# Attention scores scaled, masked and reduced a unit at a time; more sums of exponentials on ScalarE; three sums of squares on TensorE

## The chip, the cores and the metric

The kernel runs on one core of a Trainium2 chip. The metric is the device time of one execution in microseconds (us). A measurement gives the median of several executions; one further execution is recorded by the hardware profiler, and all rows below come from that one. Five engines work at the same time, each through its own queue in order: TensorE (PE in the rows; PEld is its weight loads), VectorE (DVE), ScalarE (ACT), GpSimd (POOL) and SyncE (SP). An instruction that waits for another engine holds up everything behind it in its own queue.

## The reference

Three parts follow one another. All arithmetic is float32.

```python
scores = q @ k.T / 8                                # 4 batches, 8 heads, 576 positions, 64 wide
scores = where(mask, scores, -1e9)                  # heads 0-3: the last 32 positions
attn = exp(scores - max(scores))                    # heads 4-7: same position modulo 32, not later
attn = attn / (sum(attn) + 1e-9)
x = attn @ v                                        # reshaped to 2304 tokens x 512

xn = x / sqrt(mean(x * x) + 1e-6) * rms_g
x = (silu(xn @ w_gate) * (xn @ w_val)) @ w_out      # 512 -> 1536 -> 512, weights in float64

logits = x @ w_gate2 + modality_bias[modality_id]   # 8 experts, the largest logit picks one
out = gate * (relu(x @ w1[e]) @ w2[e])              # 512 -> 1024 -> 512 for each token's expert
```

## The kernel before

Attention is cut into 48 *units*, numbered from one here. A unit is one batch, one pair of heads and two to four *tiles* of 128 rows (64 queries of each head). In each batch six strided units (heads 4 to 7; tiles of 54 keys; 4, 4 and 3 tiles) come first, then six local ones (heads 0 to 3; tiles of 96 keys; 4, 4, 3, 3, 2 and 2 tiles). A unit goes through four functions. `scores` multiplies on TensorE (L168), scales, masks and takes the row extremum on VectorE (L178, one instruction a tile, each with a readout of the extremum), and exponentiates on ScalarE (L188, one a tile). `norm` sums the exponentials on VectorE (L205; from the 13th unit on, ScalarE's exponential also gives the sum), adds 1e-9 (L206), takes the reciprocal (L207) and multiplies (L208). `transpose` goes through TensorE and ScalarE (L214, L216), and `output` multiplies by v (L224) and copies into x (L233, L239). The values are kept negated, so that the extremum is a minimum.

The feed-forward part works on nine *chunks* of 256 tokens. `rms` squares the chunk on ScalarE (L299), adds the four 128-channel parts on VectorE (L303, L304), sums over channels on TensorE against a column of ones (`root`, L317), finds the reciprocal root with a dozen small VectorE instructions (L323 to L331), spreads it (L337, L339) and scales x (L349 to L353). Then come the gate and value products (L456 to L458), the activation (L464 to L470) and the output product (L481 to L483), for each chunk and each of twelve blocks `f`.

The 36 float64 weight blocks are *converted* on the chip, numbered from one here. Each is loaded by ScalarE's queue (L379); one conversion then takes a copy on ScalarE (L387), a sign step on GpSimd (L389), two VectorE steps (L396, L400), a cast on ScalarE (L408) and a subtraction on VectorE (L409). Buffers are passed on from block to block, so that GpSimd's step of a conversion waits until L396 of the one before has read its block: L389 and L396 form a loop.

The first 24 units and the chunks are put together by hand: the program runs units until eight outputs are done, then `rms` of the first chunk, then a *flow* of (chunk, block) steps, first chunk one alone for three steps, then chunks one and two in turn, then the others. Between the steps come `slot` calls, which hand out one weight load, one conversion half and one piece of attention. What order the instructions then have on each engine is decided by a scheduler that goes by estimated durations, up to the last part (the experts), whose order is written out by hand. In the first 50 us short filler products (L117) run on TensorE as well.

Of the kernel before, what the change touches and what calls it, by code (L numbers as in the profile page):

```python
# [15 lines left out]
AF = mybir.ActivationFunctionType  # L16
# [30 lines left out]
def moe_kernel(  # L47
# [53 lines left out]
    def bank(tag, bufs=1):  # L101
        return ps.tile([128, 512], F32, tag=tag, name=tag, bufs=bufs)
# [8 lines left out]
    n_load = [0, 0]  # L111
    n_out = [0]

    def fill(dst, n):

        for _ in range(n):
            T.matmul(dst, ones16, ones16, start=True, stop=True)  # L117
# [29 lines left out]
    def attention(u, banks):  # L147

        b, p, g = units[u]
        local = p < 2  # L150
        n, t0, nq, nk = geometry(u)
        k0 = n * nq if local else n * nq + LQ - SQ
        st = {}

        def scores():
            t = qkv_t.pop((u, 0))
            pr = pp.tile([128, 4, LK], F32, tag="pr", name="pr", bufs=3)
            mx = sm.tile([128, 4], F32, tag="mx", name="mx")
            sd = sm.tile([128, 4], F32, tag="sd", name="sd")
            sps = banks("s")  # L160
            if n_fill[0] < 16:
                n_fill[0] += 1
                fill(sps[:, 384:], 10)
            sps = sps[:, :4 * LK].rearrange("p (t k) -> p t k", k=LK)
            for i in range(n):
                for h in range(2):
                    hp = slice(64 * h, 64 * h + 64)
                    T.matmul(  # L168
                        sps[hp, i, :nk],
                        t[hp, i * nq:i * nq + LQ],  # L170
                        t[hp, k0 + i * nq:k0 + i * nq + nk],
                        start=True,
                        stop=True,
                    )
            for i in range(n):
                mask = m_str if not local else (m_loc0 if g == 0 and i == 0 else m_loc)
                pv = pr[:, i, :nk]
                V.tensor_tensor_reduce(  # L178
                    out=pv,
                    in0=sps[:, i, :nk],  # L180
                    in1=mask[:, :nk],
                    op0=ALU.add,
                    op1=ALU.min,
                    scale=-0.125,
                    scalar=3.0e38,
                    accum_out=mx[:, i:i + 1],
                )
                act = A.activation(  # L188
                    out=pv,
                    in_=pv,  # L190
                    func=AF.Exp,
                    bias=mx[:, i:i + 1],
                    scale=-1.0,
                    accum_out=None if u < 12 else sd[:, i:i + 1],
                )
                if not flow_on:
                    mark[0] = act
            st["p"] = pr, sd
            load_part(0)

        def norm():
            pr, sd = st["p"]
            pv, sl = pr[:, :n, :nk], sd[:, :n]
            if u < 12:
                V.tensor_reduce(out=sl, in_=pv, op=ALU.add, axis=AX.X)  # L205
            V.tensor_scalar(out=sl, in0=sl, scalar1=1e-9, scalar2=None, op0=ALU.add)  # L206
            V.reciprocal(out=sl, in_=sl)  # L207
            V.tensor_tensor(out=pv, in0=pv, in1=sl.unsqueeze(2).to_broadcast([128, n, nk]), op=ALU.mult)  # L208

        def transpose():  # L210
            pr, _ = st.pop("p")
            pt = banks("t").rearrange("p (t k) -> p t k", k=128)
            for i in range(n):
                T.transpose(pt[:nk, i], pr[:, i, :nk], ident)  # L214
            ptS = st["t"] = pp.tile([128, 4, 128], F32, tag="ptS", name="ptS", bufs=2)
            A.copy(ptS[:nk, :n], pt[:nk, :n])  # L216

        def output():
            t = qkv_t.pop((u, 1))
            ptS = st.pop("t")  # L220
            ot = banks("o")
            for i in range(n):
                for h in range(2):
                    T.matmul(  # L224
                        ot[64 * h:64 * h + 64, i * nq:(i + 1) * nq],
                        t[:nk, i, 64 * h:64 * h + 64],
                        ptS[:nk, i, 64 * h:64 * h + nq],
                        start=True,
                        stop=True,
                    )  # L230
            if local:
                x = x_t[b, p, g] = xt_p.tile([128, n * LQ], F32, tag=f"x{g}", name=f"x{g}", bufs=2)
                A.copy(x, ot[:, :n * LQ])  # L233
            else:
                if g == 0:
                    x_t[b, p] = xt_p.tile([128, S], F32, tag="xs", name="xs", bufs=4)
                x = x_t[b, p].rearrange("p (j c) -> p c j", c=CLS)
                c0, c1 = 3 * t0, min(3 * (t0 + n), CLS)
                A.copy(x[:, c0:c1], ot[:, :(c1 - c0) * LEN].rearrange("p (c j) -> p c j", j=LEN))  # L239
            load_part(1)  # L240
            n_out[0] = u + 1


        if local and b > 0:
            output.after = (S * (b - 1) + LQ * (t0 + n) - 1) // CH
        elif not local and b > 1:
            output.after = (S * (b - 1) - 1) // CH
        return scores, norm, transpose, output
# [42 lines left out]
    def rms(j):  # L291

        st = {}
# [5 lines left out]
                    A.activation(out=sq[:, p % 2, o:o + n], in_=src, func=AF.Square)  # L299

        def add():
            sq = [st.pop(("s", q)) for q in range(2)]
            V.tensor_tensor(out=sq[0], in0=sq[0], in1=sq[1], op=ALU.add)  # L303
            V.tensor_tensor(out=sq[0][:, 0], in0=sq[0][:, 0], in1=sq[0][:, 1], op=ALU.add)  # L304
            st["sq"] = sq[0][:, 0]
# [6 lines left out]
        def root():  # L312


            ss = bank("mx") if j else bank("gv", 2)
            for m in range(2):
                T.matmul(  # L317
                    ss[:, m:m + 1], st["sq"][:, m * 128:(m + 1) * 128], ones[:, 0:1], start=True, stop=True
                )
            a = sm.tile([128, 2], F32, tag="na", name="na")  # L320
            r = sm.tile([128, 2], F32, tag="nr", name="nr")
            t = sm.tile([128, 2], F32, tag="nt", name="nt")
# [814 lines left out]
def _constants():  # L1137
    c = np.zeros((128, 6, 128), np.float32)
    r, k = np.arange(128)[:, None], np.arange(128)[None, :]
    q = r % LQ  # L1140
    loc = (k > q) & (k <= q + WIN)
    c[:, 0] = np.where(loc & (k >= WIN), 0, -8e9)
    c[:, 1] = np.where(loc, 0, -8e9)
    c[:, 2] = np.where((q // LEN == k // LEN) & (k <= q), 0, -8e9)
    c[:, 3] = np.eye(128)
    c[:, 4] = 1
    c[:, 5] = r < k
    i = np.zeros((128, NCOL + 2 * E + 1), np.float32)
    i[:, :NCOL] = np.arange(NCOL)
    i[:, NCOL:NCOL + E] = np.arange(E) * NT  # L1150
    i[:, NCOL + E] = np.arange(1, 129)
    n = r // 32 * E
    i[:, NCOL + E + 1:] = r % 32 == n + np.arange(E)
    return [c.reshape(128, -1), i]
# [82 lines left out]
```

## Time and profile before

| | |
|---|---|
| median of 3 executions | 892.23 us (891.48 to 894.1) |
| the profiled execution, its time | 890.73 us |
| span from its first to its last instruction | 889.0 us |
| busy: PE, DVE, ACT, POOL | 855.3, 532.3, 401.1, 129.4 us |
| mean granted TensorE clock, as a share of 2.4 GHz | 0.976 |

Busy times are shares of the whole span and hide that stages differ, so the rows below are cut by stretch. Between the profiled time and its span lie 1.7 us; the profiled execution is 1.5 us under the median.

### The profile page before, as it was taken

Reading aid. Unit: us, or ns where it says so; the run is one execution under the profiler, and the core shown is the slowest. Engines: PE = TensorE matmul, PEld = TensorE weight load, DVE = VectorE, ACT = ScalarE, POOL = GpSimd, SP = SyncE. Lnnn points to the kernel's source line nnn. Section 1 sums busy time; section 2 is a strip of 40 time slices with the busy share of each in tenths; the row PEclk is TensorE's granted clock in tenths of the full one; section 3 lists DMA queues with packets and bytes.
Section 4 is the critical chain, followed back from the end, with each engine's and each line's share of the span. In section 5 each row is a group of like instructions: output and inputs, shape, how many; then the busy total and the mean of one; then the engine's idle time right before and its main releaser. Section 6 shows DMA issues by size and latency. Waiting matters only on the chain.

```text
span 889.0 us, 18174 instructions
## 1 busy us (share of the span) xinstructions
PE 855.3 (96%) x6912; PEld 770.8 (87%) x6912; DVE 532.3 (60%) x1650; ACT 401.1 (45%) x971; POOL 129.4 (15%) x86
## 2 busy tenths in 40 slices
PE   8569899999999999999999999999999999999996
PEld 7458799999898889888989999998999999999995
DVE  4899999456463564553543635447596666666651
ACT  4665777334454344433232322225365545544540
POOL 1466455000000000000000000001031111111100
PEclk9759999999999999999999999999999999999998
DMA  6936611002211111200000000005187742775000
GB/s 196 361 114 261 229 51 52 10 6 71 61 45 48 40 29 36 68 24 8 25 10 24 1 1 25 1 25 213 42 323 228 223 154 83 231 222 189 25 25 19
DMA packets 33015, 84.47 MB, mean 95 GB/s; under 512 B 5122, under 2 KB 12850, under 8 KB 32920
## 3 DMA queue, kind: packets, MB, share of 16 engines
q1 hardware_dynamic: 24216, 54.89, 19.8%
q10 hardware_dynamic: 5184, 18.88, 5.7%
q0 software_dynamic: 3520, 9.45, 3.2%
q8 instruction: 58, 0.95, 0.5%
q14 instruction: 37, 0.30, 0.1%
HBM read 91.58 MB, written 10.49 MB: 115 GB/s over the span
## 4 chain that ended last, share of the span: by engine, by line
PE 72%; issue 9%; DMA 5%; DVE 3%; POOL 1%; SPq 0%; ACT 0%; POOLq 0%; DVEq 0%
PE gv L456 11%; PE gv L457 11%; PE gv L458 10%; DMA stg<-in 5%; PE o L481 4%; PE o L483 4%; PE o L482 4%; PE o L998 3%; PE o L1000 3%; PE o L999 3%; PE mx L224 2%; PE s L168 2%; PE s L975 1%; PE s L974 1%; PE s L976 1%
## 5 line engine op out<-in xcount | busy, mean ns | idle before, releaser
L456 PE MATMUL gv<-xh,wf 128*128 128x256 f32 x864 | 249.5, 290 | 1.7 <-DVE t L466 1.2
L457 PE MATMUL gv<-xl,wf 128*128 128x256 f32 x864 | 245.1, 284 | 0.0
L458 PE MATMUL gv<-xh,wf 128*128 128x256 f32 x864 | 244.8, 283 | 0.0
L456 PEld LDWEIGHTS gv<-xh,wf 128*128 128x128 f32 x864 | 163.2, 189 | 9.2 <-DVE t L466 1.8
L457 PEld LDWEIGHTS gv<-xl,wf 128*128 128x128 f32 x864 | 163.3, 189 | 3.9 <-issue 0.2
L458 PEld LDWEIGHTS gv<-xh,wf 128*128 128x128 f32 x864 | 163.6, 189 | 0.3
L941 DVE TENSOR_TENSOR l<-stg,h 128x1024 fp32r<-128x1024 f32 x88 | 107.1, 1223 | 37.3 <-ACT h L940 37.1
L465 DVE SCALAR_TENSOR_TENSOR t<-t,gv 128x256 f32<-128x256 f32 x108 | 45.1, 418 | 115.5 <-ACT t L464 114.8
L940 ACT CAST h<-stg 128x1024 fp32r<-128x1024 f32 x88 | 91.6, 1048 | 35.1 <-PE o L1000 25.9
L464 ACT ACTIVATE t<-gv 128x256 f32<-128x256 f32 x108 | 41.3, 382 | 143.0 <-PE gv L458 131.6
L389 POOL TENSOR_SCALAR wk<-raw 128x512 int32<-128x512 f32 x36 | 78.5, 2179 | 77.9 <-DVE wk L396 27.1
L481 PE MATMUL o<-wf,hh 128*128 128x512 f32 x192 | 76.9, 401 | 1.2 <-ACT hh L469 1.2
L482 PE MATMUL o<-wf,hh 128*128 128x512 f32 x192 | 75.9, 395 | 0.0
L483 PE MATMUL o<-wf,hl 128*128 128x512 f32 x192 | 75.3, 397 | 0.2 <-DVE hl L470 0.2
L469 ACT CAST hh<-t 128x256 fp32r<-128x256 f32 x108 | 43.7, 405 | 69.0 <-PE o L483 29.9
L998 PE MATMUL o<-h,hT 128*128 128x512 f32 x176 | 70.6, 401 | 0.0
L1000 PE MATMUL o<-h,hT 128*128 128x512 f32 x176 | 68.8, 391 | 0.0
L999 PE MATMUL o<-l,hT 128*128 128x512 f32 x176 | 68.5, 389 | 0.0
L924 POOL DMA_INDIRECT xg<-rows_d,gi x22 | 24.3, 1105 | 301.7 <-DMA stg<-in 141.2
L470 DVE TENSOR_TENSOR hl<-t,hh 128x256 fp32r<-128x256 f32 x108 | 47.1, 436 | 34.8 <-ACT hh L469 34.4
L188 ACT ACTIVATE pr<-pr,mx 128x54 f32<-128x54 f32 (+1 forms) x160 | 52.5, 346 | 19.3 <-DVE mx L178 17.3
L974 PE MATMUL s<-xh,h 128*128 128x256 f32 x176 | 49.7, 282 | 0.0
(208 smaller groups left out, 1636.3 us busy)
## 6 DMA issues: line engine op xcount, KB each, us to landing
stg<-in SPq DMA_DIRECT2D x96, 512.0 KB
raw<-in ACTq DMA_DIRECT2D x36, 512.0 KB
rows_d<-x SPq DMA_DIRECT2D x18, 256.5 KB
qk<-in SPq DMA_DIRECT2D x16, 221.0 KB
qk<-in SPq DMA_DIRECT2D x8, 272.0 KB
v<-in SPq DMA_DIRECT2D x16, 108.0 KB
qk<-in SPq DMA_DIRECT2D x8, 208.0 KB
v<-in SPq DMA_DIRECT2D x8, 192.0 KB
```

What stands on the lines that cost most here:

```text
L389: G.tensor_scalar(out=wk[:, 1], in0=raw[:, :, 1].bitcast(F32), scalar1=0.0, scalar2=-(2.0**31), op0=ALU.is_lt, op1=ALU.mult,)
L456: T.matmul(dst, wh[:, ks], xh[k], start=(k == order[0]), stop=False)
L457: T.matmul(dst, wh[:, ks], xl[k], start=False, stop=False)
L458: T.matmul(dst, wl[:, ks], xh[k], start=False, stop=(k == order[3]))
L481: T.matmul(o, h[:, ms], wh, start=(f == 0), stop=False)
L482: T.matmul(o, h[:, ms], wl, start=False, stop=False)
L483: T.matmul(o, l[:, ms], wh, start=False, stop=(f == NF - 1))
L940: A.copy(h, lt["stg", i])
L941: V.tensor_tensor(out=l, in0=lt["stg", i], in1=h.bitcast(F32), op=ALU.subtract)
L998: T.matmul(ys[t][m], hh, w[0][:, c], start=(q == 0 and c == 0), stop=False)
L999: T.matmul(ys[t][m], hh, w[1][:, c], start=False, stop=False)
L1000: T.matmul(ys[t][m], hl, w[0][:, c], start=False, stop=(q == 3 and c == 1))
```

## The change

Three edits:

- `scores`: scaling and masking is one VectorE instruction for all tiles of a unit that share a mask (two for the first local unit of each pair of heads), and the row minima of the unit are one further instruction. No instruction a tile with readout is left. The mask tables hold 1e9 instead of -8e9 accordingly.
- `norm`: ScalarE's exponential also gives the sum from the seventh unit on (before, from the 13th), and L205 goes for the seventh to twelfth unit. From the seventh unit on the 1e-9 is added by ScalarE instead of VectorE.
- `rms`: for the first three chunks the VectorE additions go, and TensorE sums the four parts, with four products for each half of the chunk in place of one.

```diff
+    NRED = 6
...
+            m0 = 1 if local and g == 0 else 0
+            for i0, i1, mask in ((0, m0, m_loc0), (m0, n, m_loc if local else m_str)):
+                if i0 < i1:
+                    V.scalar_tensor_tensor(
+                        out=pr[:, i0:i1, :nk], in0=sps[:, i0:i1, :nk], scalar=-0.125,
+                        in1=mask[:, :nk].unsqueeze(1).to_broadcast([128, i1 - i0, nk]),
+                        op0=ALU.mult, op1=ALU.add,
+                    )
+            V.tensor_reduce(out=mx[:, :n], in_=pr[:, :n, :nk], op=ALU.min, axis=AX.X)
             for i in range(n):
-                mask = m_str if not local else (m_loc0 if g == 0 and i == 0 else m_loc)
                 pv = pr[:, i, :nk]
-                V.tensor_tensor_reduce(
-                    out=pv,
-                    in0=sps[:, i, :nk],
-                    in1=mask[:, :nk],
-                    op0=ALU.add,
-                    op1=ALU.min,
-                    scale=-0.125,
-                    scalar=3.0e38,
-                    accum_out=mx[:, i:i + 1],
-                )
...
-                    accum_out=None if u < 12 else sd[:, i:i + 1],
+                    accum_out=None if u < NRED else sd[:, i:i + 1],
...
-            if u < 12:
+            if u < NRED:
                 V.tensor_reduce(out=sl, in_=pv, op=ALU.add, axis=AX.X)
-            V.tensor_scalar(out=sl, in0=sl, scalar1=1e-9, scalar2=None, op0=ALU.add)
+                V.tensor_scalar(out=sl, in0=sl, scalar1=1e-9, scalar2=None, op0=ALU.add)
+            else:
+                A.activation(out=sl, in_=sl, func=AF.Copy, bias=1e-9)
...
         def add():
+            if j < 3:
+                return
...
+            if j < 3:
+                sq = [st["s", q][:, i] for q in range(2) for i in range(2)]
+            else:
+                sq = [st["sq"]]
             for m in range(2):
-                T.matmul(
-                    ss[:, m:m + 1], st["sq"][:, m * 128:(m + 1) * 128], ones[:, 0:1], start=True, stop=True
-                )
+                for i, a in enumerate(sq):
+                    T.matmul(
+                        ss[:, m:m + 1], a[:, m * 128:(m + 1) * 128], ones[:, 0:1],
+                        start=(i == 0), stop=(i == len(sq) - 1),
+                    )
```

The scheduler orders the changed program anew, most of all on VectorE and ScalarE in the first 100 us. In the rows below, line numbers of the changed kernel are its own: L181 and L186 are the new scaling and minima, L209 is ScalarE's addition of 1e-9; L210, L211, L398, L407, L411, L419, L420 and L334 are L207, L208, L387, L396, L400, L408, L409 and L323 of before.

On VectorE, where the tenth to twelfth unit are normalized and the fifth and sixth conversion pass, there stands before, from L400 of the fifth conversion to L396 of the sixth:

```order
L400 SCALAR_TENSOR_TENSOR wk<-wk 128x512
L207 RECIPROCAL sd<-sd 128x3
L409 TENSOR_TENSOR wf<-wk,wf 128x512
L206 TENSOR_SCALAR sd<-sd 128x2
L208 TENSOR_TENSOR pr<-pr,sd 128x288
L205 TENSOR_REDUCE sd<-pr 128x2
L207 RECIPROCAL sd<-sd 128x2
L396 SCALAR_TENSOR_TENSOR wk<-raw,wk 128x512
```

and now, from L407 of the fifth conversion to that of the sixth:

```order
L407 SCALAR_TENSOR_TENSOR wk<-raw,wk 128x512
L210 RECIPROCAL sd<-sd 128x3
L211 TENSOR_TENSOR pr<-pr,sd 128x288
L210 RECIPROCAL sd<-sd 128x2
L211 TENSOR_TENSOR pr<-pr,sd 128x192
L411 SCALAR_TENSOR_TENSOR wk<-wk 128x512
L420 TENSOR_TENSOR wf<-wk,wf 128x512
L210 RECIPROCAL sd<-sd 128x2
L211 TENSOR_TENSOR pr<-pr,sd 128x192
L420 TENSOR_TENSOR wf<-wk,wf 128x512
L407 SCALAR_TENSOR_TENSOR wk<-raw,wk 128x512
```

L396 of the sixth conversion stood ahead of the subtraction (L409) of the fifth and of the last reciprocal; now L407 stands behind all reciprocals and products of these units and behind the subtractions of the fourth and the fifth.

On ScalarE, in the same place, there stands before, from the last load of a group to the cast after the 12th unit's exponentials:

```order
L379 DMA raw<-in 128x1024 x3
L188 ACTIVATE pr<-pr,mx 128x96 x2
L408 CAST wf<-wk 128x512
L387 ACTIVATE wk<-raw 128x512
L188 ACTIVATE pr<-pr,mx 128x96 x2
L233 COPY x_656<-mx 128x256
L216 COPY ptS<-o_783 96x384
L408 CAST wf<-wk 128x512
```

and now, from the 11th unit's last exponential to the next cast but one:

```order
L189 ACTIVATE pr,sd<-pr,mx 128x96
L209 ACTIVATE sd<-sd 128x2
L189 ACTIVATE pr,sd<-pr,mx 128x96
L398 ACTIVATE wk<-raw 128x512
L419 CAST wf<-wk 128x512
L236 COPY x_641<-mx 128x256
L219 COPY ptS<-o_769 96x384
L209 ACTIVATE sd<-sd 128x2
L398 ACTIVATE wk<-raw 128x512
L419 CAST wf<-wk 128x512
```

The copy of the sixth conversion (L387) stood ahead of the 12th unit's exponentials; now the copies of the fifth and of the sixth (L398) both stand behind them. The reciprocal on VectorE now waits for L209, which for the 12th unit stands behind a conversion's copy and cast and two other copies.

On VectorE, where the squares of the first chunk are added, there stands before:

```order
L400 SCALAR_TENSOR_TENSOR wk<-wk 128x512
L409 TENSOR_TENSOR wf<-wk,wf 128x512
L396 SCALAR_TENSOR_TENSOR wk<-raw,wk 128x512
L303 TENSOR_TENSOR sq<-sq 128x512
L400 SCALAR_TENSOR_TENSOR wk<-wk 128x512
L304 TENSOR_TENSOR sq<-sq 128x256
L178 ISA pr,mx<-pt,cs 128x54
L178 ISA mx 128x1
...
L409 TENSOR_TENSOR wf<-wk,wf 128x512
L396 SCALAR_TENSOR_TENSOR wk<-raw,wk 128x512
L323 TENSOR_SCALAR na<-gv 128x2
```

and now, up to the same small instruction of `root`:

```order
L407 SCALAR_TENSOR_TENSOR wk<-raw,wk 128x512
L411 SCALAR_TENSOR_TENSOR wk<-wk 128x512
L420 TENSOR_TENSOR wf<-wk,wf 128x512
L407 SCALAR_TENSOR_TENSOR wk<-raw,wk 128x512
L181 SCALAR_TENSOR_TENSOR pr<-pt,cs 128x4x54
L411 SCALAR_TENSOR_TENSOR wk<-wk 128x512
L186 TENSOR_REDUCE mx<-pr 128x4
L420 TENSOR_TENSOR wf<-wk,wf 128x512
L407 SCALAR_TENSOR_TENSOR wk<-raw,wk 128x512
L334 TENSOR_SCALAR na<-gv 128x2
```

The two additions are gone, and between the last two conversions ahead of `root` two instructions of the 13th unit stand in place of eight. On TensorE the sum over channels is four rows of L317 for each of the first three chunks before and sixteen now.

## Rows read from the trace of the kernel before

**Rows 1.** Busy time by stretch: PE, PEld, DVE, ACT, POOL, granted clock, DMA share, GB/s

```profile
25.00:50.00 25.00, 13.30 (x157) 10.92 (x158) 20.25 (x75) 16.67 (x44) 12.60 (x6) 0.67 0.97 352
...
75.00:100.00 25.00, 21.87 (x184) 18.91 (x183) 24.20 (x64) 15.95 (x39) 15.20 (x7) 1.00 0.67 257
...
125.00:150.00 25.00, 25.00 (x230) 22.55 (x230) 23.65 (x63) 18.26 (x52) 14.42 (x7) 1.00 0.17 48
```

**Rows 2.** Timeline of PE: start us, us, operation, idle before and releaser

```profile
50.18 1.23 PE L117 MATMUL pt<-ones 128*128 128x128 bf16 x10 [4.93 <-ACT ptS L216]
...
53.41 1.02 PE L317 MATMUL gv<-cs,sq 128*128 128x1 f32 x4 [0.97 <-DVE sq L304]
...
76.45 0.38 PE L456 MATMUL gv<-xh,wf 128*128 128x256 f32 x1 [0.91 <-DVE t L466]
...
102.09 0.39 PE L456 MATMUL gv<-xh,wf 128*128 128x256 f32 x1 [0.33 <-DVE t L466]
```

**Rows 3.** Timeline of DVE: maxima of a unit and sums of exponentials

```profile
8.28 0.21 DVE L178 CUSTOM_DVE_ANT_0 pr<-s,cs 128x54 f32<-128x54 f32 x1
8.41 0.08 DVE L178 DVE_READ_ACCUMULATOR2_ANT mx<- 128x1 f32 x1
8.41 0.21 DVE L178 CUSTOM_DVE_ANT_0 pr<-s,cs 128x54 f32<-128x54 f32 x1
...
18.86 0.37 DVE L205 TENSOR_REDUCE sd<-pr 128x4 f32<-128x216 f32 x1
...
30.13 0.55 DVE L205 TENSOR_REDUCE sd<-pr 128x4 f32<-128x384 f32 x1
30.59 0.17 DVE L207 RECIPROCAL sd<-sd 128x4 f32<-128x4 f32 x1
```

**Rows 4.** Groups by shape: busy us, mean ns, idle before and releaser

```profile
L465 DVE SCALAR_TENSOR_TENSOR t<-t,gv 128x256 f32<-128x256 f32 x108 | 45.1, 418 | 115.5 <-ACT t L464 114.8
...
L206 DVE TENSOR_SCALAR sd<-sd 128x4 f32<-128x4 f32 x24 | 4.5, 189 | 8.0 <-ACT pr L188 7.9
```

**Rows 5.** Timeline of DVE around the squares of the first chunk

```profile
51.28 0.68 DVE L303 TENSOR_TENSOR sq<-sq 128x512 f32<-128x512 f32 x1
...
52.94 0.41 DVE L304 TENSOR_TENSOR sq<-sq 128x256 f32<-128x256 f32 x1
...
54.41 0.68 DVE L396 SCALAR_TENSOR_TENSOR wk<-raw,wk 128x512 int32<-128x512 int32 x1
55.01 0.15 DVE L323 TENSOR_SCALAR na<-gv 128x2 f32<-128x2 f32 x1
```

**Rows 6.** Instructions of L317 in the first chunk: duration min/median/max, starts

```profile
L317 PE MATMUL gv<-cs,sq x4: 352/353/373, 53.4 to 54.1; 128*128 128x1 f32 x4
```

**Rows 7.** Timeline of PE: the same sum of squares in the third chunk

```profile
178.73 0.50 PE L317 MATMUL mx<-cs,sq 128*128 128x1 f32 x4
179.09 0.36 PE L456 MATMUL gv<-xh,wf 128*128 128x256 f32 x1
```

**Rows 8.** Timeline of POOL: its step of the sixth to ninth conversions

```profile
39.53 1.94 POOL L389 TENSOR_SCALAR wk<-raw 128x512 int32<-128x512 f32 x1 [1.04 <-DVE sd L206]
44.27 2.29 POOL L389 TENSOR_SCALAR wk<-raw 128x512 int32<-128x512 f32 x1 [2.79 <-DVE wk L396]
48.25 2.39 POOL L389 TENSOR_SCALAR wk<-raw 128x512 int32<-128x512 f32 x1 [1.69 <-DVE wk L396]
51.51 2.27 POOL L389 TENSOR_SCALAR wk<-raw 128x512 int32<-128x512 f32 x1 [0.87 <-DVE wk L396]
```

**Rows 9.** Timeline of ACT between 40 and 54 us

```profile
40.48 0.64 ACT L188 ACTIVATE pr<-pr,mx 128x96 f32<-128x96 f32 x2 [1.70 <-DMA raw<-in]
...
48.20 0.67 ACT L387 ACTIVATE wk<-raw 128x512 f32<-128x512 f32 x1 [1.42 <-DVE wk L396]
...
53.58 0.34 ACT L188 ACTIVATE pr<-pr,mx 128x54 f32<-128x54 f32 x1
...
53.91 0.32 ACT L188 ACTIVATE pr<-pr,mx 128x54 f32<-128x54 f32 x1
```

More of the change, by code (lines that the diff above doesn't have):

```diff
@@ L1141, in _constants @@
     loc = (k > q) & (k <= q + WIN)
-    c[:, 0] = np.where(loc & (k >= WIN), 0, -8e9)
-    c[:, 1] = np.where(loc, 0, -8e9)
-    c[:, 2] = np.where((q // LEN == k // LEN) & (k <= q), 0, -8e9)
+    c[:, 0] = np.where(loc & (k >= WIN), 0, 1e9)
+    c[:, 1] = np.where(loc, 0, 1e9)
+    c[:, 2] = np.where((q // LEN == k // LEN) & (k <= q), 0, 1e9)
     c[:, 3] = np.eye(128)
```

## Prediction

> **What bounds the kernel now.** I read the table of stretches first: it says in which part of the span a saving can count at all. From 125 us on TensorE is busy for the whole of each stretch up to 570 us, the first of which stands here, and VectorE, though busy for 23.65 of 25 us between 125 and 150 us, holds nobody up [rows 1]. Only TensorE's own work has a price there. Between 75 and 100 us VectorE is busy for 24.20 of 25 us and TensorE for 21.87: here VectorE sets the pace [rows 1]. Between 25 and 50 us neither is full; the DMA engines are, at 0.97 of their share [rows 1]. So a VectorE saving must fall before about 102 us, where the timeline of TensorE has its last idle time: from 53.41 to 102.09 us eleven rows of that view begin after an idle time, the first of 0.97 us, the last of 0.33 us, 7.7 us in all [rows 2]. That is the most that the stretch of the flow can give back; the 4.93 us before 50.18 us come on top and belong to the head [rows 2].
>
> The second thing to see is what the head waits for. ScalarE's queue is held by weight loads until 40.48 us and by a VectorE step of a conversion at 48.20 us [rows 9], and the conversions form a loop with GpSimd: its steps start at 39.53, 44.27, 48.25 and 51.51 us, and the idle time before the last three ends with VectorE's L396 [rows 8]. The shortest of these periods, 3.26 us, is about GpSimd's 2.3 us and L396's 0.68 us with hand-overs [rows 5, 8], so I take it as the loop's floor. The first small step of the first chunk's root (L323, 55.01 us) stands directly behind the ninth conversion's L396, which begins at 54.41 us [rows 5].
>
> **The change part by part.** The sum is made against the profiled execution, 890.73 us, 1.50 us under the median.
>
> *Maxima.* Two tiles' instructions start 0.13 us apart, and the readout between them takes no time of its own [rows 3]: four tiles of 54 cost 0.53 us. A reduction of 384 columns hands over after 0.46 us although it lasts 0.55, so 0.09 us are a tail that overlaps; that of 216 columns, 0.37 us, then costs 0.28 us [rows 3]. The new scaling reads PSUM and SBUF as L465 does, 0.418 us for 256 columns [rows 4]; 40 columns less at the (0.55 - 0.37) / 168 = 1.07 ns of the reductions give 0.375 us, 0.29 us without the tail. So a strided unit of four tiles costs 0.57 us instead of 0.53, one of three 0.46 instead of 0.39; a local unit of four 0.9 to 1.0 instead of 0.70 (a tile of 96 is 0.13 us plus 42 columns, 0.175 us). The edit adds VectorE time, because every column is now read twice. In the VectorE-bound stretch (65 to 102 us) three units are scored: +0.2 us.
>
> The Trainium skill (Vector Engine (DVE) Microarchitecture Reference, Measured stream behaviour on trn2) states about 75 ns for each instruction after queue overlap and 1.0417 ns a column. By it the readouts, of one column each, would cost 76 ns apiece, and eleven of them in this stretch would make the edit save 0.6 us instead of costing 0.2, and the total 0.8 us less. The trace disagrees on the readouts, whose start coincides with that of the next tile [rows 3], and agrees on the slope with 1.07 ns.
>
> *Sums.* Six L205 of the seventh to twelfth unit go, 0.46 us and less each [rows 3], all in the head, where VectorE is not full. ScalarE pays for them: two exponentials with sums start 0.33 us apart for 54 columns [rows 9], and eighteen of the tiles now have sums. By the slope above a local one costs some 0.36 us. The addition of 1e-9 leaves VectorE for 42 units: 0.189 us long, less the tail 0.10 us [rows 4]; four of them between 65 and 102 us, -0.4 us.
>
> *Squares.* VectorE is spared 0.59 + 0.32 us, the two rows without their tails, for each of three chunks [rows 5]. TensorE gets twelve more passes a chunk. At full clock four take 179.09 - 178.73 = 0.36 us [rows 7], so twelve cost 1.08 us; in the first chunk four starts spread over 0.7 us [rows 6], at the half clock that the page's slices show there, and twelve cost 2.5 us or a little less.
>
> *Head, up to the first gate product.* Here the order decides. Before, ScalarE left its wait at 40.48 us and GpSimd's seventh step began at 44.27 us, 3.8 us later [rows 8, 9]. The new order puts one chain between them: four exponentials with sums (1.44 us), three copies of sums (0.4), a load's issue (0.3), then for the fifth conversion copy, shift, cast and subtraction and for the sixth L407 (five steps of 0.6 to 0.68 us, taken like L396), together 5.4 us: GpSimd would begin at 45.9 us. From there the loop has no squares, no L205 and fewer instructions in it; I take the floor: steps at 49.1 and 52.4 us, the ninth L407 2.3 us later, at 54.7 us instead of 54.41. The sixteen passes over the first chunk are not later than that: the last square comes some 0.5 us earlier than before, since one conversion less stands ahead of it, and seven products of two passes take 2.9 us. Head: +0.3 us. Bounds: all lateness kept, +1.6 us; or the two long periods before (4.74 and 3.98 us) shrink to the floor as well, -2.2 us. Units one to six only get latency of about 0.4 us each, under DMA that is full soon after: 0, with 1 us on either side.
>
> *Flow, 65 to 102 us.* VectorE: -0.9 (squares of chunk two) - 0.4 + 0.2 = -1.1 us. TensorE's 1.08 us for chunk two fall where it waited 0.91 us for VectorE [rows 2], and cost 0.2 us. Bounds: with the contention that stretches some VectorE rows, -2.1 us; hidden behind GpSimd's loop, 0; the passes in full, +1.1 us.
>
> *Chunk three* is squared at 178 us, where TensorE never idles: +1.1 us. Later units cost VectorE more and the chain from scores to products some 0.7 us more, but between a unit's scores and its transposes the order leaves TensorE 8 us and more of other work; 0, and that is what would pay if the cover went.
>
> Sum: 0 + 0.3 - 1.1 + 0.2 + 1.1 = +0.5 us, that is 891.2 us profiled and 892.7 us as a median. The low ends add up to -4.2 us, the high ends to +4.8 us.
>
> **The rivals.** All times are medians.
>
> *Faster: the loop runs at its floor.* VectorE no longer stands in wait for exponentials ahead of a reduction, and if ScalarE is not the later one, both long periods shrink (-2.2), the flow gives -2.1 with the extra passes hidden, and chunk three takes 1.1 back: -3.2 us, 889.0 us. For it speaks that all idle time before GpSimd's steps ended with VectorE [rows 8]; against it, that the new order moves the fifth and sixth copies on ScalarE behind the exponentials.
>
> *Slower: ScalarE becomes the bound of the head.* ScalarE is busy for 16.67 us between 25 and 50 us and held by loads besides [rows 1, 9], and gets some 2.5 us more. A reciprocal then waits for a tiny copy behind a cast, and the conversion's step stands behind the reciprocal. The 1.6 us stay, the passes of chunks two and three cost 2.2 us in full, and the flow gains nothing: +3.8 us, 896.0 us. It decides if GpSimd's seventh step begins later than about 46 us.
>
> *The edit on VectorE doesn't do what it says.* By the prices above, eight instructions fewer a unit are no time saved; in all 48 units the maxima cost VectorE some 8 us more than before. That is in the forecast; by the rule on instructions it would be 0.8 us better, the same case.
>
> **How the numbers follow.** About 0.3% (2.7 us) is what a measurement of this kernel can tell from no change, so "no change" means 889.6 to 894.9 us. I give it 0.38, the faster rival 0.33 and the slower 0.29: the terms are small and of both signs, and the order of the first 60 us, which no row of before shows, can move the result by several us either way. The likeliest case by itself is 890 to 895 us. The range that leaves out a tenth on either side reaches past both rivals, near the sums of the ends: 887.8 to 897.0 us.
>
> **What would show it.** Right: L181 of 216 columns lasts about 0.37 us and VectorE's total changes little; GpSimd's seventh step at 45 to 46.5 us and L334 within 1 us of 55; TensorE's idle time after 53 us down by about 1 us; 1.4 us for the sixteen passes of chunk three. Wrong: TensorE's clock back at full well before or after the slices in which it was before, idle time of TensorE after 102 us, L407 waiting for ScalarE in every period, or loads that land elsewhere because ScalarE issues them in another order.

## The result, and the profile after

The changed kernel takes 898.79 us (median of 4 executions, 898.41 to 901.5) against 892.57 us for the kernel before, measured beside it: a ratio of 1.0078 with a 95% interval of 1.0057 to 1.0098. A second series gave 899.89 against 892.67 us, 1.0086 [1.0068, 1.0104]. Taken from the ratios, as all differences of runs below, that is 7.0 and 7.7 us slower (the medians differ by 6.2 and 7.2). The forecast was 892.7 us, its range 887.8 to 897.0 us: the measured time lies above it. The two profiled executions stand further apart than the medians, 901.5 and 890.73 us: the changed kernel's lies 2.7 us above its median, that of before 1.8 us under. So differences between single rows are read with some 4 us in mind, and what is held against them comes from several runs.

The table of stretches of the changed kernel answers to [rows 1]; its columns are the same.

```profile
75.00:100.00 25.00, 23.79 (x189) 21.66 (x189) 22.18 (x54) 14.61 (x37) 14.71 (x7) 1.00 0.66 257
100.00:125.00 25.00, 21.31 (x179) 19.18 (x178) 21.54 (x46) 15.64 (x51) 12.61 (x7) 0.86 0.53 185
```

Between 75 and 100 us TensorE is now busy for 23.79 us instead of 21.87, as VectorE's relief was to bring. But between 100 and 125 us it is busy for 21.31 us (before: 23.46) at a granted clock of 0.86 (before: 1.00). The first small step of each chunk's root, a fixed place in the program, tells how late the kernel is. On the timeline of VectorE these are, for chunks one to three:

```profile
57.94 0.15 DVE L334 TENSOR_SCALAR na<-gv 128x2 f32<-128x2 f32 x1
81.85 0.15 DVE L334 TENSOR_SCALAR na<-mx 128x2 f32<-128x2 f32 x1
189.07 0.16 DVE L334 TENSOR_SCALAR na<-mx 128x2 f32<-128x2 f32 x1 [0.77 <-PE mx L327]
```

In the trace of before they begin at 55.01 [rows 5], 79.02 and 179.27 us, and that of chunk four at 249.94 us (now 260.32). The changed kernel is 2.9 us late at chunk one, 2.8 at chunk two, 9.8 at chunk three and 10.4 at chunk four. The traces show two losses, then: 2.9 us in the head, and 7 us between 82 and 189 us. TensorE's timeline (start, us, operation, idle before and releaser) answers to [rows 2] and shows both:

```profile
52.56 3.15 PE L327 MATMUL gv<-cs,sq 128*128 128x1 f32 x14
...
73.06 0.41 PE L469 MATMUL gv<-xh,wf 128*128 128x256 f32 x1
78.81 1.84 PE L327 MATMUL mx<-cs,sq 128*128 128x1 f32 x16
...
95.62 0.28 PE L469 MATMUL gv<-xh,wf 128*128 128x256 f32 x1
...
104.24 0.56 PE L170 MATMUL pt<-qk 64*64 64x54 f32 x12 [1.66 <-DVE pr L181]
106.83 0.58 PE L467 MATMUL gv<-xh,wf 128*128 128x256 f32 x1 [2.03 <-DVE t L477]
107.64 0.41 PE L467 MATMUL gv<-xh,wf 128*128 128x256 f32 x1
...
187.20 1.84 PE L327 MATMUL mx<-cs,sq 128*128 128x1 f32 x16
```

Counted are the gate and value products that read xh. The fifth, at 73.06 us, began at 69.50 us before: 3.6 us late. The 93rd is only 2.5 us late (100.87 against 98.36 us), the 97th 4.7 us (106.83 against 102.09 [rows 2]), behind two idle times of 1.66 and 2.03 us, and from there a product takes 0.41 us in place of 0.28. Short stretches show the clock (columns as in the table above):

```profile
102.00:106.00 4.00, 1.14 (x34) 0.88 (x29) 3.67 (x8) 1.29 (x3) 3.12 (x2) 0.95 0.69 206
106.00:110.00 4.00, 3.17 (x15) 3.17 (x16) 2.95 (x8) 3.19 (x13) 0.53 (x1) 0.50 1.01 385
110.00:114.00 4.00, 4.00 (x21) 3.65 (x21) 3.81 (x9) 1.76 (x5) 2.01 (x2) 0.70 0.94 358
```

TensorE was busy for 1.14 of the 4 us from 102 us on, and then got the half clock, 1.2 GHz: (0.05 + 0.50 + 0.30) x 4 = 3.4 us of full clock gone. Before, the clock was 1.00 throughout this stretch. What TensorE waited for is L477, the end of a block's activation. VectorE's queue ahead of it:

```profile
100.06 0.69 DVE L407 SCALAR_TENSOR_TENSOR wk<-raw,wk 128x512 int32<-128x512 int32 x1 [1.57 <-POOL wk L400]
...
103.20 0.69 DVE L407 SCALAR_TENSOR_TENSOR wk<-raw,wk 128x512 int32<-128x512 int32 x1 [0.29 <-POOL wk L400]
103.81 0.38 DVE L181 SCALAR_TENSOR_TENSOR pr<-pt,cs 128x216 f32<-128x216 f32 x1
104.10 1.12 DVE L420 TENSOR_TENSOR wf<-wk,wf 128x512 fp32r<-128x512 f32 x1
105.15 0.41 DVE L476 SCALAR_TENSOR_TENSOR t<-t,gv 128x256 f32<-128x256 f32 x1
105.48 0.68 DVE L411 SCALAR_TENSOR_TENSOR wk<-wk 128x512 int32<-128x512 int32 x1
106.08 0.36 DVE L186 TENSOR_REDUCE mx<-pr 128x4 f32<-128x216 f32 x1
106.37 0.41 DVE L477 TENSOR_TENSOR t<-t,gv 128x256 f32<-128x256 f32 x1
```

The activation (L476, L477) stands behind L407 of the 21st conversion, which waits for GpSimd, and L420 of the 20th, and L411 of the 21st stands between its two steps. In the trace of before the 20th's subtraction (L409) has begun at 99.55 us, ahead of the activation, and one step of the 21st (L396) stands between the two:

```profile
100.16 0.41 DVE L465 SCALAR_TENSOR_TENSOR t<-t,gv 128x256 f32<-128x256 f32 x1
...
101.02 0.68 DVE L396 SCALAR_TENSOR_TENSOR wk<-raw,wk 128x512 int32<-128x512 int32 x1
101.63 0.41 DVE L466 TENSOR_TENSOR t<-t,gv 128x256 f32<-128x256 f32 x1
```

In the changed kernel the activation's first step on ScalarE stands behind the cast of the 20th conversion:

```profile
102.44 0.62 ACT L419 CAST wf<-wk 128x512 fp32r<-128x512 f32 x1 [0.82 <-DVE wk L411]
102.96 0.38 ACT L475 ACTIVATE t<-gv 128x256 f32<-128x256 f32 x1
```

Of the head, GpSimd's sixth to ninth step, ScalarE ahead of the seventh and around the last square (answers to [rows 8, 9]), and VectorE directly ahead of the root's first step:

```profile
44.61 2.45 POOL L400 TENSOR_SCALAR wk<-raw 128x512 int32<-128x512 f32 x1 [4.10 <-ACT wk L398]
48.32 2.39 POOL L400 TENSOR_SCALAR wk<-raw 128x512 int32<-128x512 f32 x1 [1.26 <-DVE wk L407]
51.59 2.39 POOL L400 TENSOR_SCALAR wk<-raw 128x512 int32<-128x512 f32 x1 [0.87 <-DVE wk L407]
54.85 1.95 POOL L400 TENSOR_SCALAR wk<-raw 128x512 int32<-128x512 f32 x1 [0.87 <-DVE wk L407]
```

```profile
41.53 0.37 ACT L189 ACTIVATE pr<-pr,mx 128x96 f32<-128x96 f32 x1 [0.99 <-DMA qk<-in]
...
42.63 0.33 ACTq L390 DMA_DIRECT2D raw<-in  x1
43.06 0.38 ACT L189 ACTIVATE pr<-pr,mx 128x96 f32<-128x96 f32 x1 [0.62 <-DVE sd L210]
...
51.52 0.68 ACT L398 ACTIVATE wk<-raw 128x512 f32<-128x512 f32 x1 [1.32 <-issue]
52.11 0.40 ACT L302 ACTIVATE sq<-x 128x256 f32<-128x256 f32 x1
```

```profile
57.34 0.68 DVE L407 SCALAR_TENSOR_TENSOR wk<-raw,wk 128x512 int32<-128x512 int32 x1
```

The loop does run at its floor from the seventh step on (3.27 and 3.26 us), but that step comes at 48.32 us (before: 44.27, forecast: 45.9), and the last square now stands behind a conversion's copy.

### The profile page after: what moved, and what is told of

The parts are those of the page before. It is cut to its first block, busy times and chain, and to the rows that moved or that the text cites. A ratio compares the mean times of both kernels' runs of the same rounds, so it can differ in the third digit from the quotient of the medians.

```text
span 899.4 us, 17989 instructions
## 1 busy us (share of the span) xinstructions
PE 867.2 (96%) x6948; PEld 781.5 (87%) x6948; DVE 529.6 (59%) x1380; ACT 406.2 (45%) x1031; POOL 129.1 (14%) x86
## 4 chain that ended last, share of the span: by engine, by line
PE 75%; issue 9%; DMA 1%; POOL 1%; DVE 1%; SPq 0%; ACT 0%; POOLq 0%; DVEq 0%
PE gv L467 11%; PE gv L468 11%; PE gv L469 10%; PE o L494 5%; PE o L492 5%; PE o L493 4%; PE o L1009 3%; PE o L1011 3%; PE o L1010 3%; PE mx L227 2%; PE s L170 2%; PE s L985 2%; PE s L986 2%; PE s L987 2%; PE gv L985 2%
## 5 line engine op out<-in xcount | busy, mean ns | idle before, releaser
L476 DVE SCALAR_TENSOR_TENSOR t<-t,gv 128x256 f32<-128x256 f32 x108 | 45.3, 419 | 110.5 <-ACT t L475 109.6
L400 POOL TENSOR_SCALAR wk<-raw 128x512 int32<-128x512 f32 x36 | 77.8, 2160 | 83.7 <-DVE wk L407 28.7
```

## The experiments

All ratios are to the kernel before, measured beside it, with a 95% interval. In the diffs a line with - is of the kernel that the text names as the base; they are shortened, and `...` marks what is left out.

**One edit alone.** Base: the kernel before. The first theory was that ScalarE's new work costs (A), the rival that VectorE's new order and double reading do (B).

```diff
+V.scalar_tensor_tensor(out=pr[:, i0:i1, :nk], in0=sps[:, i0:i1, :nk], scalar=-0.125, ...)
+V.tensor_reduce(out=mx[:, :n], in_=pr[:, :n, :nk], op=ALU.min, axis=AX.X)
...
-V.tensor_tensor_reduce(out=pv, in0=sps[:, i, :nk], in1=mask[:, :nk], ...)
```

> The kernel before with the maxima edit alone (one scaling and one reduction a unit). Theory A (ScalarE's new work is what costs): this edit adds nothing to ScalarE, so the first full run of gate products starts within 1 us of before (69.5 us in the trace) and the time within 0.3% of before, +0.2 to +0.6 us. Theory B (the new order on VectorE is what costs, every column being read twice there): two thirds of the loss are here, +4 us or more, with gate products 2 us or more later than before.

Measured: 893.15 us, 1.0002 [0.999, 1.0014]. No difference: theory B fell. The fifth of the products that read xh begins at 71.28 us, 1.8 us late, between what the two theories expected. VectorE is busy for 539.3 us instead of 532.3, so the edit does cost it time, 7 us where the forecast had some 8 for all units, but none that counts.

```diff
+NRED = 6
...
-accum_out=None if u < 12 else sd[:, i:i + 1],
+accum_out=None if u < NRED else sd[:, i:i + 1],
...
-if u < 12:
+if u < NRED:
     V.tensor_reduce(out=sl, in_=pv, op=ALU.add, axis=AX.X)
-V.tensor_scalar(out=sl, in0=sl, scalar1=1e-9, scalar2=None, op0=ALU.add)
+    V.tensor_scalar(out=sl, in0=sl, scalar1=1e-9, scalar2=None, op0=ALU.add)
+else:
+    A.activation(out=sl, in_=sl, func=AF.Copy, bias=1e-9)
```

> The kernel before with the sums edit alone (sums of the 7th to 12th unit by the exponential, 1e-9 added by ScalarE from the 7th unit on). Theory A: most of the loss is here, +3.5 to +6 us; VectorE's reciprocal of the 8th or 9th unit waits 2 us or more for ScalarE's addition, and the gate products start 2.5 to 4 us later than before. Theory B: VectorE has less to do and nothing is lost, -1 to +1 us.

Measured: 891.1 us, 0.9994 [0.9981, 1.0008]. Theory A fell: no loss.

```diff
+if j < 3: return
...
+sq = [st["s", q][:, i] for q in range(2) for i in range(2)]
```

> The kernel before with the squares edit alone (sixteen passes of TensorE for each of the first three chunks, no additions on VectorE). Both theories: head and gate start as before within 1 us; +1.1 us for chunk three, +0.2 to +1.1 for chunk two, -0.9 to 0 for VectorE's additions: +0.3 to +2.2 us. If a third cause is at work, TensorE held by passes in the stretch where it runs at half clock, gate products start 1 us or more later and the time is +3 us or more.

Measured: 897.98 us, 1.0065 [1.005, 1.0081], +5.8 us. Both theories fell, and the clause on a third cause was met in its numbers (the fifth product begins at 73.37 us, 3.9 us late): the squares edit carries the loss. That passes at the half clock are this cause isn't shown by it; the runs by chunk below speak against it.

**The changed kernel again**, unchanged.

> The changed kernel once more, for a second profile: the profiled execution lay 2.7 us above the other three. If the second stretch of half clock (105.6 to 112.4 us) comes with the order of instructions, it is there again and the time is 898 to 899 us or more; if it hangs on the one execution, TensorE's idle time of 1.7 and 2.0 us at 104 and 107 us or the half clock behind it is gone in this profile, and its span is 896 to 897 us.

Measured: 899.89 us. The second half-clock stretch is there again, from 105.1 to 111.9 us, and the idle times are 1.66 and 2.04 us: they come with the order.

**The squares edit taken back.** Base: the changed kernel.

```diff
-if j < 3:
+if j < 0:
```

> The changed kernel with the squares edit alone taken back (maxima and sums edits stay). If the squares edit is the whole cause, whatever stands beside it, the 7.2 us go: 892 to 893.5 us, and the gate products start within 1.5 us of before. If the edits only cost together (three edits crowd ScalarE and VectorE in the head), half of the loss or more stays, 896 us or more.

Measured: 893.63 us, 1.0013 [1.0002, 1.0023]. The loss goes but for 1.2 us, and the fifth product begins at 69.35 us, as before. Of the two other edits together that is what stays. Where it arises wasn't followed up; the trace has a granted clock of 0.61 between 101 and 105 us, where that of before has 1.00.

**Squares by chunk.** Base: the kernel before with the squares edit for all three. Theory C put the loss on the first chunk's passes, theory D on chunks two and three.

```diff
-if j < 3:
+if j == 0:
```

> The kernel before with the squares edit for the first chunk alone. Theory C (the twelve more passes of the first chunk stand on the head's chain at half clock, and the root's small steps then fall behind conversions): +3 to +4.5 us, with the spreading product and the gate products 3.5 to 4.5 us later than before. Theory D (the loss is the price of the passes where TensorE never idles, chunks two and three): -0.5 to +1 us.

Measured: 893.46 us, 1.0011 [1.0002, 1.002]. The gate products are 4.8 us late in the trace, but the time is only 1.0 us up (3.3 us between the two profiled executions): lateness in the head doesn't stand in the time in full.

```diff
-if j < 3:
+if j in (1, 2):
```

> The kernel before with the squares edit for the second and third chunk alone. Theory C: the rest, +1 to +2.5 us, of which 1.1 to 1.9 at the third chunk. Theory D: +4 us or more, with the gate products of the first chunk starting as before.

Measured: 899.51 us, 1.0086 [1.0073, 1.0099]. Theory C fell.

For the first chunk alone, with the halves added on VectorE (base: the run of the first chunk alone):

```diff
+V.tensor_tensor(out=sq[0], in0=sq[0], in1=sq[1], op=ALU.add)
...
-sq = [st["s", q][:, i] for q in range(2) for i in range(2)]
+sq = [sq[0][:, i] for i in range(2)]
```

> As the run before last (squares edit for the first chunk alone), but VectorE adds the two halves and TensorE makes eight passes instead of sixteen. If the number of passes sets the lateness, 8 passes fewer at 0.2 us each: 1.4 to 1.9 us less lateness of the root than with sixteen, and the time 1 to 2.5 us over before. If it is the new order of VectorE's small steps that costs, the lateness doesn't go by the number: it is as with sixteen passes or gone.

Measured: 892.94 us, 1.0004 [0.9989, 1.0018], not to be told from the sixteen passes or from before: a miss for the numbers expected, and too small an effect to split. The root's first step begins at 57.91 us, with sixteen passes at 57.63 us: its lateness doesn't go by the number of passes.

```diff
-if j < 3:
+if j == 2:
```

> The kernel before with the squares edit for the third chunk alone, where TensorE never idles. If twelve passes cost there what they last (sixteen starts 1.59 us apart in the changed kernel's trace against four 0.25 us apart), +1.3 us. If something else hangs on the third chunk (VectorE spared two additions there, the orders behind it), the time differs from that by more than 1 us.

Measured: 893.58 us, 1.0012 [1.0, 1.0025], +1.1 us, near the passes' own length (1.34 us by the rows).

```diff
-if j < 3:
+if j == 1:
```

> The kernel before with the squares edit for the second chunk alone. In the order of TensorE this kernel has, as the run of chunks two and three, eight of the sixteen passes ahead of a block's gate products and eight behind it. If that place is what costs, the second half starts 7 us after the first, the root's first step some 5 us later than before, TensorE idles 6 us between 75 and 100 us in place of 3.1, and the time is +4 to +6 us. If it is the passes' length alone, +1.3 us or less.

Measured: 899.54 us, 1.0081 [1.0066, 1.0097]. Twelve passes of some 0.11 us cost 7.2 us by this ratio, more than the 4 to 6 us expected of their place. The root is 5.1 us later than before, as expected, but the halves stand 5 us apart and not 7, and TensorE is idle for 3.6 of the 25 us from 75 us on, not for 6. So this run alone doesn't show that the place is the cause; one below takes the place away. The timelines of TensorE and VectorE show the two halves and the root behind the second:

```profile
76.25 0.95 PE L328 MATMUL mx<-cs,sq 128*128 128x1 f32 x8
81.40 0.95 PE L328 MATMUL mx<-cs,sq 128*128 128x1 f32 x8
```

```profile
84.10 0.15 DVE L335 TENSOR_SCALAR na<-mx 128x2 f32<-128x2 f32 x1
```

**The same chunks in the changed kernel.** Base: the changed kernel; one chunk's additions go back to VectorE.

```diff
-if j < 3:
+if j in (0, 2):
```

> The changed kernel with VectorE's additions back for the second chunk (sixteen passes for the first and third). If the idle time of TensorE near 104 to 107 us and the half clock behind it come from the order that all edits together give, they can go here: 895.5 to 897 us; if they stay, the passes of chunk two alone are saved, 1.3 us: 897.5 to 898.5 us.

Measured: 894.48 us, 1.0027 [1.0015, 1.004], +2.4 us: under both numbers expected.

```diff
-if j < 3:
+if j in (1, 2):
```

> The changed kernel with VectorE's additions back for the first chunk (sixteen passes for the second and third). If the first chunk's passes at half clock are what delays the gate products, they start 2 to 3.5 us earlier than in the changed kernel (73.1 us), and the time is 896 to 897 us; if the additions on VectorE take as long as the passes, the start moves by less than 1 us and the time by less than 1.5 us, 898 to 900 us.

Measured: 893.63 us, 1.001 [0.9996, 1.0024], +0.9 us: again under both, though the products start 2.9 us earlier, as the first theory had it. Here sixteen passes for chunks two and three cost nothing that can be measured against the run without squares (893.63 us as well, 1.0013), where by themselves they cost 7.7 us. In both of these runs TensorE's idle times at 101 to 102 us are 1.1 and 0.5 us, in place of 1.66 and 2.03. Taking either chunk back saves 4.6 to 6.8 us, so the loss isn't a sum over chunks. What the two runs share is the place of the activation in VectorE's queue, one conversion earlier than in the changed kernel: ahead of L407 of the 21st and L420 of the 20th, with L411 of the 20th between its steps. In the second of them:

```profile
100.21 0.41 DVE L476 SCALAR_TENSOR_TENSOR t<-t,gv 128x256 f32<-128x256 f32 x1
...
101.55 0.41 DVE L477 TENSOR_TENSOR t<-t,gv 128x256 f32<-128x256 f32 x1
...
103.28 0.68 DVE L407 SCALAR_TENSOR_TENSOR wk<-raw,wk 128x512 int32<-128x512 int32 x1
```

Two runs change a place in the queues alone.

**One activation moved.** Base: the changed kernel. Explicit orders put four instructions of two conversions behind the activation of the second chunk's first block; the diff writes them out for the 20th and the 21st conversion.

```diff
+with tc.issue_after(tanh.ins):
+    A.activation(out=wk21[:, 0].bitcast(F32), ...)
+    A.copy(w20[:, 0], wk20)
+with tc.issue_after(last_product.ins):
+    V.scalar_tensor_tensor(out=wk21[:, 1], in0=raw21[:, :, 0], ...)
+    V.tensor_tensor(out=w20[:, 1], in0=wk20, in1=w20[:, 0].bitcast(F32), op=ALU.subtract)
```

> The changed kernel with one order forced: the activation of the second chunk's first block goes ahead of the 20th conversion's copy and the 21st's first steps on ScalarE and VectorE, ahead of which it stands in none of the changed kernel's orders; up to there VectorE's order is the same. Theory E (one conversion more ahead of that activation is what opens TensorE's 3.7 us of idle time at 102 to 107 us, and the half clock behind it follows from that idle time): the idle time falls to 2 us or less, the products of the next block start 3 us or more earlier, the half clock is shorter or gone, and the time is 893.5 to 896.5 us. Theory F (only the passes' length and the late head cost): 898 us or more, as without it.

Measured: 894.32 us, 1.0023 [1.0012, 1.0035], +2.1 us: 4.9 and 5.6 us under the two series of the changed kernel. VectorE's queue is the same up to 102.5 us, then (L485 and L486 are the activation):

```profile
102.60 0.38 DVE L181 SCALAR_TENSOR_TENSOR pr<-pt,cs 128x216 f32<-128x216 f32 x1
102.90 0.41 DVE L485 SCALAR_TENSOR_TENSOR t<-t,gv 128x256 f32<-128x256 f32 x1
103.22 0.37 DVE L186 TENSOR_REDUCE mx<-pr 128x4 f32<-128x216 f32 x1
103.51 0.41 DVE L486 TENSOR_TENSOR t<-t,gv 128x256 f32<-128x256 f32 x1
```

On TensorE the idle times are 0.65 and 0.39 us (the second on its timeline), and the table of short stretches has the full clock:

```profile
103.98 0.39 PE L476 MATMUL gv<-xh,wf 128*128 128x256 f32 x1 [0.39 <-DVE t L486]
```

```profile
102.00:106.00 4.00, 2.96 (x43) 2.71 (x39) 3.58 (x11) 1.57 (x5) 0.95 (x1) 1.00 0.79 278
106.00:110.00 4.00, 4.00 (x31) 3.71 (x30) 1.90 (x5) 3.91 (x16) 1.68 (x1) 1.00 1.04 392
```

Theory E held in its numbers but for one: the products of the next block begin 2.85 us earlier (103.98 against 106.83 us), not 3 us or more. The root of chunk three begins at 183.14 us, 5.9 us earlier than in the changed kernel.

**The passes kept together.** Base: the kernel before with the squares edit for chunk two alone (899.54 us).

```diff
+with tc.high_priority() if j == 1 else ExitStack():
+    for m in range(2):
+        for i, a in enumerate(sq): T.matmul(ss[:, m:m + 1], ...)
```

> The kernel before with the squares edit for the second chunk alone, as in the run that took 899.5 us, but with the sixteen passes given precedence, so that none stands behind a block's gate products. If the place of the second eight is what cost 7 us there, the root's first step is again within 1.5 us of before (79 us) and the time 892 to 894.5 us. If it is something else about the second chunk's passes, 897 us or more stay.

Measured: 893.74 us, 1.0018 [1.0005, 1.0031], +1.6 us; 5.6 of the 7.2 us were the place. The root's first step is even 2.8 us earlier than before, outside the 1.5 us expected:

```profile
70.89 0.85 PE L329 MATMUL mx<-cs,sq 128*128 128x1 f32 x4
72.59 2.55 PE L329 MATMUL mx<-cs,sq 128*128 128x1 f32 x12
```

```profile
76.19 0.15 DVE L336 TENSOR_SCALAR na<-mx 128x2 f32<-128x2 f32 x1
```

**Looking for a better version.** Bases: the changed kernel, and the kernel before with the sums edit; the squares edit for chunk two alone.

```diff
-if j < 3:
+if j == 1:
```

> The maxima and sums edits with the squares edit for the second chunk alone (the run without the first chunk's passes, less the third's too). If the third chunk's passes cost 1.1 to 1.3 us, as by themselves, 892.3 us (891.5 to 893), no more than before.

Measured: 892.83 us, 1.0002 [0.9989, 1.0015], as expected and no gain.

> The sums edit with the squares edit for the second chunk alone, the two that can help by themselves (sums -0.5 to -1.5 us; the second chunk's passes in the one order in which they helped). If gains add up, 889.5 to 891 us, faster than before; if the second chunk's passes again cost by the order that comes out, 893 us or more.

Measured: 894.56 us, 1.0017 [1.0003, 1.0031]: gains don't add up, and the second clause was met. No version was shown to beat the kernel before; the sums edit alone comes nearest.

## Why the prediction was wrong

*Maxima (+0.2 us): right.* L181 of 216 columns lasts 0.36 to 0.38 us in the rows shown (forecast 0.375), L186 0.36; alone the edit makes no difference. The price of an instruction in the Trainium skill (Vector Engine (DVE) Microarchitecture Reference, Measured stream behaviour on trn2), about 75 ns, gives an estimate 0.8 us better than that by the rows. The interval of the run, -0.9 to +1.2 us, can't tell the two apart.

*Sums (-0.4 us): right*, -0.5 us with 0 in the interval. The slower rival had the direction and its sign, GpSimd's seventh step after 46 us, and in the head ScalarE is waited for: the sixth step stands idle for 4.10 us until its copy (44.61 us). But this isn't what costs: with the sums edit alone the seventh step begins at 46.34 us, and nothing is lost.

Both together cost 1.2 us, so the zero for later units, whose chain from scores to products the forecast had 0.7 us longer, may be short of that; no run takes it alone. The faster rival's loop at its floor came true from the seventh step on only; the step before it began 3.71 us earlier, so the long periods ahead did not shrink to the floor.

*Head (+0.3 us): too low.* Up to 69 us VectorE's order is the same in four runs (the changed kernel, its second series, and the runs with the second chunk taken back and with one activation moved), and the order of before is the same in five. The root's first step begins at 56.22 to 57.94 us (mean 57.4) in the four against 55.01 to 56.47 (mean 55.8) in the five: +1.6 us, the upper bound. The clause on the passes held: the last square comes 0.7 us later on the mean, not 0.5 earlier, but fourteen passes behind it take 3.15 us (forecast 2.9) and end at 55.7 us, 1.6 us before the ninth L407 begins, and directly behind that stands the root's first step. What was mis-sized is the chain ahead of the loop. ScalarE leaves its wait at 41.53 us, and at 40.50 to 40.82 us in the other three (forecast 40.48). From there to GpSimd's seventh step it takes 6.8 us (until 48.32 us), 6.1 to 7.5 us over the four, not 5.4, and a load's issue that the sum had at 0.3 us stops ScalarE for 0.62 us here (43.06 us), for 1.13 and 1.32 us in two others. From the seventh step to the ninth L407 it takes 9.0 us, near the 8.8 forecast. Without the squares edit the seventh step begins at 46.65 us, and with the second chunk taken back at 46.59 us; but without it the root's first step stands ahead of the ninth L407 and begins at 54.65 us, with it behind at 56.22 us. So 1.6 us come with the place that the squares edit gives to this step. By the run of the first chunk alone, 1.0 us up, not all of such lateness stays in the time.

*Flow (-1.1 + 0.2 us): the step that failed.* Up to 101 us it came as forecast: the lateness falls from 3.6 to 2.5 us although 1.34 us of passes were added. The sum took it that time spared on VectorE stays spared to the end of the stretch. It doesn't: the freed queue was filled in another order, with the steps of one conversion more ahead of and inside one activation for which TensorE waits. With that order undone the traces move by 5.9 us and the time by 4.9 to 5.6 us. By the rows, the idle times account for 2.65 us (1.66 + 2.03 against 0.65 + 0.39 us). The half clock behind them accounts for some 2.4 us: the block's gate and value products begin 2.85 us later than with the order undone, the output products behind them 5.22 us later (112.12 against 106.90 us). The two weren't tried apart. The prediction named idle time of TensorE after 102 us as a sign of error, but gave it no price, so neither the sum of the high ends nor the range had room for it. The kernel before itself has such a wait (0.33 us at 102.09 us [rows 2]); what an instruction more ahead of L466 would cost there could have been read.

*Passes of chunks two and three (+0.2 and +1.1 us).* Sixteen last 1.84 us, the four of before 0.50 us: 1.34 us a chunk, 0.11 us a pass rather than 0.09. At chunk three that is the loss (+1.1 us alone); at chunk two the place of the passes decides between 0 and 7 us.

In sum: passes 2.7 us and the activation's place 4.9 to 5.6 us; with it undone 2.1 us are left (1.1 to 3.1 by the interval), so that flow and head together gave some 0.6 us back, which the interval can't tell from nothing. That is the 7.0 to 7.7 us measured, where the forecast had +0.5.

## What to carry to other kernels

Where in-order queues are filled by a scheduler, a sum of durations prices an edit only if the new order is read as well, at every place where the bounding engine still waits: what stands ahead of the instruction that it waits for, before and now. The steps of one conversion more ahead of one activation cost more here than all durations in the sum. And an edit measured in one order isn't measured: the same twelve passes cost 7.2 us, 1.6 us or nothing; force the order of two or three instructions to tell the edit from its place.

## What was unexpected of the hardware

A short wait was paid twice on TensorE: after idle times of 1.66 and 2.03 us with 0.56 us of work between them its products ran at the half clock (starts 0.213 us apart instead of 0.118) until 112.4 us, and in the second profile, after 1.66 and 2.04 us, until 111.9 us. With idle times of 0.65 and 0.39 us at the same place the clock stayed at 1.00. Between these the idle times alone don't decide it. After 1.06 and 0.48 us the run with the second chunk taken back got 0.57 between 102 and 106 us; after 1.07 and 0.48 us that with the first chunk taken back kept 1.00:

```profile
102.00:106.00 4.00, 3.83 (x19) 3.83 (x20) 2.58 (x8) 3.19 (x13) 0.66 (x2) 0.57 1.01 353
```

```profile
102.00:106.00 4.00, 3.99 (x30) 3.81 (x31) 2.58 (x7) 3.34 (x13) 0.66 (x2) 1.00 1.02 376
```

Likewise after 1.38 and 0.33 us the run of the third chunk alone got 0.57 between 104 and 108 us, and the kernel before kept 1.00. So a profile's clock behind such a wait is that of one execution.

GpSimd's step beside VectorE's L364 took 3.78 us in place of 1.95 to 2.6 us, and pushed VectorE's next L407 back by 1.57 us of idle time (100.06 us in the rows above). In the trace of before the step beside the same two subtractions (L353, from 93.45 us on) took 2.29 us:

```profile
96.24 3.78 POOL L400 TENSOR_SCALAR wk<-raw 128x512 int32<-128x512 f32 x1 [3.03 <-DVE wk L407]
```

```profile
93.67 2.29 POOL L389 TENSOR_SCALAR wk<-raw 128x512 int32<-128x512 f32 x1 [3.29 <-DVE wk L396]
```

The Trainium skill (GPSIMD Engine Reference, Specifications) says that GpSimd shares its SBUF interfaces with VectorE and contends with instructions that have two SBUF inputs. Both L364 and L353 have two, so this rule by itself doesn't give the 3.78 us; no run took L364 away, and the cause stays open.

With one order on VectorE, the head still moved by 1.7 us between runs (root at 56.22 and 57.94 us). In the earliest of the four the load's issue ahead of ScalarE's third exponential begins at 40.89 us and stops nothing; in the others it begins at 42.31 to 42.63 us, and ScalarE stands idle for 0.62 to 1.32 us.
